# A spectral-filter and Swish kernel: PSUM of the first batch's transform split into five buffers, its stages interleaved per unit, and the second batch moved to other steps

## The chip, the cores and the metric

The kernel runs on one core of a Trainium2 chip. The metric is the device time of one execution in microseconds (us). PE is TensorE, DVE is VectorE, ACT is ScalarE, POOL is GpSimd, SP is SyncE (here it only issues DMAs). Ratios are the mean time of one kernel's fast runs over that of the other kernel's fast runs of the same rounds on the same chip, so they are not quite the ratio of the medians that are quoted beside them. A profile shows one execution; its span is a little shorter than the time of the run.

## The reference, cut to what matters

```python
x:      (8, 3008, 256)          # batch, sequence, channels
filt_r, filt_i: (1505, 256)
w_in:   (256, 2048); w_out: (2048, 256); beta: (2048,)

X = rfft(x, axis=1);  Y = X * (filt_r + 1j*filt_i);  y = irfft(Y, n=3008, axis=1)
h = y.reshape(24064, 256) @ w_in
g = h / (1 + exp(-beta * h))
out = g @ w_out
```

The kernel does both Fourier transforms as matmuls with 3008 = 47 x 64: a stage s1 over 47, a stage s2 over 64, the product with the filter, and the same back (s3, s4).

## The kernel before

The main loop has 752 steps. Each step does two matmuls of the hidden layer (`hps`), the Swish on ACT (`gT`), and, two steps later, four matmuls of the output layer (`acc`). Batch 0 is transformed ahead of the loop ("the setup"). Batches 1 to 7 are transformed inside the loop, their stages spread over the steps by a plan:

```python
first_step = [(S * b // TB) * NFB for b in range(B)] + [NSTEP]     # 0, 80, 176, ...
def at(s, fn, *a):
    plan.setdefault(int(s), []).append((fn, a))
...
if b == 1:                                       # o = 0
    s1_steps(1, range(8, 16), [o + 1 + i for i in range(8)], False)
    for g in range(NH): at(o + 10 + 2 * g, turn_t3, g)
    for g in range(NG): at(o + 12, a2_load, 1, g)
    s23_steps(1, [o + r for r in (20, 23, 26, 29, 33, 36, 39, 42, 45, 50, 53, 56)], 5, True)   # s3 five steps after s2
    for h in range(J // JG): at(o + 64, zz_load, 1, h)
    s4_steps(1, [o + 71 + i // 2 for i in range(16)], True)
    for f in (2, 3):
        at(f, load_wout, f * WG)                 # DMA, issued on SP
        at(f, scale_wout, f * WG)                # POOL
    for g in range(NH): at(4, copy_fr, g)        # two POOL copies each: filt_r on all partitions
    for g in range(4): at(o + 10 + 3 * g, load_x, 2, g)           # DMA, issued on POOL
    late = (57, 58, 59, 60, 61, 62, 66, 67, 68, 69, 70, 71, 72, 73, 74, 75)
    s1_steps(2, range(16), [o + r for r in late], False)
```

The kernel sets a manual schedule, so each engine's instructions stand in the order of the program, and a step of the plan is also a place in each engine's line (POOL's line in the timelines below stands in that order).

```python
def s1(b, i, on_act):            # every fourth unit takes a new a1 tile from a pool of two
    ...
    evac(st["a1", b][:, jj : jj + 2, :], ps[:KP], on_act)          # then a1_store: DMA on SP
def s2(b, i):
    ps, ks = s2_matmuls(b, i)
    nc.vector.tensor_tensor(a_t[:], ps[:], fr_sb[:, ks, :], ALU.mult)          # reads copy_fr's result
    nc.vector.scalar_tensor_tensor(b_t[:M], ps[M:], -1.0, ff_sb[M:, ks, :], ALU.mult, ALU.mult)
    nc.vector.tensor_tensor(b_t[M:], ps[:M], ff_sb[M:, ks, :], ALU.mult)
    nc.gpsimd.tensor_tensor(yh[:], a_t[:], b_t[:], ALU.add)                    # POOL
# s3(b, i): PE multiplies yh; s4 writes y of the batch, which hps reads
```

In the setup, PSUM is one ring of four two-bank buffers, whatever the stage: transposes ("turns"), the two products p and q of a unit (8 frequencies x 128 channels), the return stage.

```python
spsum = tile_pool(name="spsum", bufs=4, space=PSUM)
def s2_0(n):                                     # one unit: both matmul groups, then both products
    ps, pw = bank2([P, KH, P]), bank2([P, KH, P])
    ...
    nc.vector.scalar_tensor_tensor(p_t[:], ps[:], sgn[:], ff_sb[:, ks, ds], ALU.mult, ALU.mult)
    nc.vector.tensor_tensor(q_t[:], pw[:], ff_sb[:, ks, ds], ALU.mult)
```

## Time and profile before

| | before |
|---|---|
| median of 3 runs | 806.81 us (806.59 to 808.27) |
| span of the profile | 803.4 us |
| PE busy | 768.3 us, 96% |
| first `hps` pair of matmuls complete (end of the setup) | 52.4 us |

The page's line of busy times, and from its table of 40 slices (20 us each) the row of PE's busy share in tenths:

```profile
PE 768.3 (96%) x6109; PEld 551.8 (69%) x6201; DVE 448.4 (56%) x694; ACT 556.9 (69%) x807; POOL 169.4 (21%) x186
...
PE   4799997999999999999999999999999999999997
```

(Some matmul records are missing from this trace, 6109 of 6201 are there, so its PE busy time is a little low.) The profiled execution took 805.22 us at a mean clock of 0.998. PE is at 90% or more except in the first two slices (the setup), in the seventh, 120 to 140 us, and in the last. The waits of PE from 45 to 200 us, longest first; each line is who waited, for whom, the total, how often and the longest:

```profile
PE ps L619 <- DVE a L117: 2.2, 1, 2.2
PE ps L619 <- DMA zz<-d: 2.2, 1, 2.2
PE acc L730 <- DVE ost L741: 1.7, 1, 1.7
PE ps L545 <- ACT y L115: 0.9, 1, 0.9
```

Three things cost time there: `zz` (the input of s4) lands late, DVE is late behind an a1 cast (`a`), and the output tile's copy (`ost`) is late. The lines at L619 and L545, with one of 0.3 us left out, make 5.6 us between 126 and 138 us. After 160 us the waits view lists nothing for PE. The chain of waits around the largest gap, in order of time (start, length, what):

```profile
124.60 0.70 DVE a L117
...
125.65 9.93 DMA d<-a
...
135.66 0.69 DVE a L117
136.35 0.46 DVE y L119
```

A store of an a1 tile (`d<-a`) took 9.93 us; the DVE cast that needed the tile's buffer waited for it (4.6 us by DVE's waits), and the `y` of 0.46 us that PE needed stands right behind that cast in the chain, at 136.35 us. After the gaps PE is slow for a while. The windows view (stretch, busy us and instruction count of PE, PEld, DVE, ACT and POOL, granted clock, DMA share, GB/s):

```profile
137.00:138.00 1.00, 0.73 (x7) 0.47 (x5) 0.98 (x3) 0.48 (x1) 0.00 (x0) 0.85 0.19 53
138.00:139.00 1.00, 1.00 (x6) 0.54 (x5) 0.57 (x1) 0.00 (x0) 0.00 (x0) 0.50 0.02 4
141.00:142.00 1.00, 1.00 (x14) 0.71 (x12) 0.34 (x2) 0.12 (x1) 0.00 (x0) 0.95 0.00 0
```

The clock is 0.50 for about 3.4 us, and four `acc` matmuls take 0.85 us there (from 137.84 us) where they took 0.44 before the gaps (from 120.21 us): by an estimate from these two, about 1.7 us of lost work. The longest single gap of PE before it was 2.2 us; what brought the 0.50 on is not shown by this trace.

POOL's line before the second batch (start, length, what, count, idle time before it and what ended that):

```profile
52.91 3.74 POOL L348 TENSOR_TENSOR wout_sb<-ws,rbeta_sb 128x1024 bf16<-128x1024 f32 x2 [3.99 <-DMA ws<-in_moe_w_out_dram]
56.72 1.88 POOL L525 COPY fr_sb<-ff_sb 64x2048 f32<-64x2048 f32 x1
...
66.41 1.89 POOL L526 COPY fr_sb<-ff_sb 64x2048 f32<-64x2048 f32 x1
...
74.99 1.26 POOL L580 TENSOR_TENSOR yh<-a_t,b_t 128x512 bf16<-128x512 f32 x1 [2.48 <-DVE b_t L579]
```

The second pair of w_out scalings (L348) begins when its load lands at 52.9 us, the six copies follow to 68.3 us, and the first `yh` waits for DVE, not for POOL.

### The profile page before, as it was taken

How to read it: one execution, taken by the hardware profiler on the slowest of the kernel's cores; microseconds unless marked ns; L12 is line 12 of the kernel's file. 1: busy time of each engine (PE TensorE's matmuls, PEld its weight loads, DVE VectorE, ACT ScalarE, POOL GpSimd, SP SyncE). 2: the span in 40 equal slices, each digit the busy share in tenths (PEclk: the TensorE clock that was granted, in tenths of full speed). 3: DMA queues.
4: the chain of work that ended last, by engine and by line, in shares of the span. 5: the costliest groups of instructions: out<-in, count | busy, mean ns of one | idle time of the engine just before them, and what ended most of it. 6: DMA issues, size and time to landing. Idle time of an engine off the chain costs nothing.

```text
span 803.4 us, 15446 instructions
## 1 busy us (share of the span) xinstructions
PE 768.3 (96%) x6109; PEld 551.8 (69%) x6201; DVE 448.4 (56%) x694; ACT 556.9 (69%) x807; POOL 169.4 (21%) x186
## 2 busy tenths in 40 slices
PE   4799997999999999999999999999999999999997
PEld 4667664766677666776668766786667766676664
DVE  7665764476655665566655666556764666330101
ACT  4776674776667766676767676677666777777775
POOL 8157331132201322023310222011210122000000
PEclk9999999999999999999999999999999999999999
DMA  9948237523571418513293134912245111500101
GB/s 166 229 135 199 69 80 208 141 74 109 129 219 39 120 47 201 171 49 86 70 244 106 47 86 131 256 33 81 78 135 155 62 58 48 151 27 27 53 28 52
DMA packets 84187, 88.29 MB, mean 110 GB/s; under 512 B 5968, under 2 KB 75088, under 8 KB 83736
## 3 DMA queue, kind: packets, MB, share of 16 engines
q1 hardware_dynamic: 79460, 72.37, 30.2%
q0 software_dynamic: 4656, 14.95, 10.9%
q8 instruction: 48, 0.79, 0.4%
q14 instruction: 23, 0.19, 0.1%
HBM read 54.01 MB, written 46.66 MB: 125 GB/s over the span
## 4 chain that ended last, share of the span: by engine, by line
PE 90%; DMA 1%; DVE 1%; issue 1%; ACT 0%; DVEq 0%; SPq 0%; ACTq 0%
PE acc L730 42%; PE hps L710 38%; PE ps L545 3%; PE ps L590 2%; PE ps L619 2%; PE ps L561 2%; DMA d<-a 1%; DVE a L117 0%; DVE ost L741 0%; PE tp L602 0%; ACT gT L719 0%; DVE a_t L575 0%; DVE b_t L576 0%; DVE b_t L579 0%; DVEq L770 0%
## 5 line engine op out<-in xcount | busy, mean ns | idle before, releaser
L719 ACT ACTIVATE gT<-hps,beta_sb 128x512 bf16<-128x512 f32 x752 | 516.5, 687 | 219.3 <-PE hps L710 196.5
L730 PE MATMUL acc<-wout_sb,gT 128*128 128x256 bf16 x3008 | 454.2, 273 | 4.2 <-DVE ost L741 1.7
L710 PE MATMUL hps<-y,win_sb 128*128 128x512 bf16 (+7 forms) x1636 | 428.6, 350 | 1.2 <-DVE y L119 0.6
L730 PEld LDWEIGHTS <-gT 128*128 128x128 bf16 x3008 | 288.0, 98 | 128.5 <-issue 4.3
L580 POOL TENSOR_TENSOR yh<-a_t,b_t 128x512 bf16<-128x512 f32 x84 | 106.3, 1265 | 426.2 <-DVE b_t L579 419.3
L710 PEld LDWEIGHTS <-win_sb 128*128 128x128 bf16 x1728 | 164.9, 98 | 25.8 <-DVE y L119 1.3
L741 DVE COPY ost<-acc 128x512 f32<-128x512 f32 x94 | 60.5, 685 | 139.8 <-PE acc L730 139.8
L575 DVE TENSOR_TENSOR a_t<-ps,fr_sb 128x512 f32<-128x512 f32 x84 | 58.1, 692 | 75.3 <-PE ps L561 74.7
L117 DVE CAST a<-ps 96x512 bf16<-96x512 f32 x104 | 70.8, 685 | 51.5 <-PE ps L545 44.9
L119 DVE TENSOR_SCALAR y<-ps 128x376 bf16<-128x376 f32 x104 | 55.9, 547 | 61.4 <-PE ps L619 61.2
L576 DVE SCALAR_TENSOR_TENSOR b_t<-ps,ff_sb 64x512 f32<-64x512 f32 x84 | 58.2, 692 | 1.1
L579 DVE TENSOR_TENSOR b_t<-ps,ff_sb 64x512 f32<-64x512 f32 x84 | 57.4, 683 | 1.1
L117 DVE CAST z<-ps 128x512 bf16<-128x512 f32 x78 | 53.4, 684 | 1.8 <-PE ps L590 0.8
L619 PEld LDWEIGHTS <-zz 96*128 96x128 bf16 x448 | 29.5, 99 | 27.1 <-issue 3.3
L545 PE MATMUL ps<-xg,t 94*96 94x512 bf16 x104 | 40.0, 384 | 1.9 <-ACT y L115 0.9
L619 PE MATMUL ps<-t,zz 96*128 96x94 bf16 x448 | 34.4, 206 | 5.2 <-DVE a L117 2.2
L590 PE MATMUL ps<-yh,t 128*128 128x256 bf16 x168 | 32.1, 273 | 0.6
L561 PE MATMUL ps<-a,tw_sb 128*128 128x256 bf16 x168 | 32.1, 273 | 0.3
L590 PEld LDWEIGHTS <-t 128*128 128x128 bf16 x168 | 16.3, 98 | 17.7 <-issue 0.2
L335 POOL DMA_DIRECT2D xg<-in_x_dram x28 | 15.1, 539 | 62.7 <-PE ps L545 57.4
L561 PEld LDWEIGHTS <-tw_sb 128*128 128x128 bf16 x168 | 16.1, 98 | 16.3
L545 PEld LDWEIGHTS <-t 94*96 94x96 bf16 x104 | 12.9, 124 | 10.1 <-DVE b_t L579 0.4
(94 smaller groups left out, 218.3 us busy)
## 6 DMA issues: line engine op xcount, KB each, us to landing
out_dram<-ost SPq DMA_DIRECT2D x47, 512.0 KB, 3.0
d<-a SPq DMA_DIRECT2D x28, 384.0 KB, 3.3
a<-d SPq DMA_DIRECT2D x28, 384.0 KB, 5.1
d<-z SPq DMA_DIRECT2D x28, 384.0 KB, 3.7
zz<-d SPq DMA_DIRECT2D x28, 384.0 KB, 6.7
xg<-in_x_dram POOLq DMA_DIRECT2D x28, 320.0 KB, 6.2
ws<-in_moe_w_out_dram SPq DMA_DIRECT2D x4, 512.0 KB, 5.3
xg<-in_x_dram POOLq DMA_DIRECT2D x28, 56.0 KB, 6.0
```

Source lines behind the costliest of these rows:

```text
L117: nc.vector.tensor_copy(dst, src)
L545: nc.tensor.matmul(ps[:KP], lhsT=t1[:], rhs=xg[b, g][:, jj : jj + 2, :], start=True, stop=True)
L561: nc.tensor.matmul(ps[:, e, :], lhsT=t2[:, k0 + e, :], rhs=st["a2", b, g][:, kk + e, :], start=True, stop=True,)
L575: nc.vector.tensor_tensor(a_t[:], ps[:], fr_sb[:, ks, :], ALU.mult)
L576: nc.vector.scalar_tensor_tensor(b_t[:M], ps[M:], -1.0, ff_sb[M:, ks, :], ALU.mult, ALU.mult)
L580: nc.gpsimd.tensor_tensor(yh[:], a_t[:], b_t[:], ALU.add)
L590: nc.tensor.matmul(ps[:, e, :], lhsT=t3[:, 2 * i + e, :], rhs=yh[:, e, :], start=True, stop=True)
L619: nc.tensor.matmul(ps[:, e, :NP], lhsT=zz[:, j0 % JG + e, dc * P : (dc + 1) * P], rhs=t4[:], start=True, stop=True,)
L710: nc.tensor.matmul(hps[:, pos - t0 : pos - t0 + ln], lhsT=win_sb[:, dc, fb * P : (fb + 1) * P], rhs=ys[b][:, dc, n0 : n0 + ln], start=(dc ...
L719: nc.scalar.activation(gT[:], hps[:], ACT.Silu, scale=beta_sb[:, fb : fb + 1])
L730: nc.tensor.matmul(acc[tb // 2][:, tb % 2, :], lhsT=gT[:, tb * P : (tb + 1) * P], rhs=wout_sb[:, fb, :], start=(fb == 0 and tb % 2 == 0), ...
L741: nc.vector.tensor_copy(ost[:, 2 * h : 2 * h + 2, :], acc[h][:])
```

## The change

Its intent: let the setup's products on DVE follow each other by giving the short turns their own one-bank PSUM buffers and by putting a turn or a return stage between the p and the q matmuls of a unit; and let the second batch start earlier, with its s1, s2, s3, s4 and the third batch's s1 on steps that do not collide (s4 on steps 67 to 79 instead of 71 to 78), and two of its s1 casts, those of units 10 and 14, on ACT instead of DVE. The core of the diff:

```diff
-        tc.tile_pool(name="spsum", bufs=4, space=bass.MemoryType.PSUM)
+        tc.tile_pool(name="spsum", bufs=3, space=bass.MemoryType.PSUM)
+    )
+    tpsum = right.enter_context(
+        tc.tile_pool(name="tpsum", bufs=2, space=bass.MemoryType.PSUM)
...
+    def turn8():
+        return tpsum.tile([P, KH, P], BF16, name="tps", tag="tps")
...
-    s2_0(0)
-    a0_turn(1, (False, True))
-    t3_part(1, 1, True)
-    t3_part(0, 1, True)
-    s2_0(1)
-    s3_0(0)
...
+    s2_0(1, False)          # p of unit 1
+    t3_part(0, 1)
+    s2_0(1, True)           # q of unit 1
+    s3_0(0)
+    t3_part(1, 1)
+    a0_turn(2, 0, False)
...
-            s1_steps(1, range(8, 16), [o + 1 + i for i in range(8)], False)
+            s1_steps(1, range(8, 16), [o + r for r in (0, 1, 1, 2, 3, 4, 4, 5)], False, (10, 14))
...
-                at(o + 10 + 2 * g, turn_t3, g)
+                at(o + 6 + 3 * g, turn_t3, g)
-                at(o + 12, a2_load, 1, g)
-            s23_steps(1, [o + r for r in (20, 23, 26, 29, 33, 36, 39, 42, 45, 50, 53, 56)], 5, True)
+                at(o + 8, a2_load, 1, g)
+            s23_steps(1, [o + r for r in (15, 18, 21, 24, 27, 30, 34, 37, 40, 43, 46, 50)], 5, True)
-                at(o + 64, zz_load, 1, h)
-            s4_steps(1, [o + 71 + i // 2 for i in range(16)], True)
+                at(o + 59, zz_load, 1, h)
+            s4_steps(1, [o + 67 + (i * 12) // 15 for i in range(16)], True)
...
-                late = (57, 58, 59, 60, 61, 62, 66, 67, 68, 69, 70, 71, 72, 73, 74, 75)
+                late = (54, 55, 56, 57, 58, 59, 60, 61, 66, 67, 68, 70, 72, 73, 74, 76)
```

Untouched are the plan's lines for `load_wout`, `scale_wout`, `copy_fr` and `load_x` of the third batch. Two of the second batch's four-unit groups are still transformed in the setup, but four of their eight units now come after the last product instead of two of eight.

More of the change, by code (lines that the diff above doesn't have):

```diff
@@ L241, in s1_0, with a0_turn, t3_part @@
         evac(aTv[:, g], src, on_act)
-    def a0_turn(kg, acts):
-        tp = bank2([P, KH, NDC, P], BF16)
-        ks = slice(kg * KH, (kg + 1) * KH)
+    def a0_turn(kg, e, on_act):
+        tp = turn8()
         for kk_ in range(KH):
-            for e in range(NDC):
-                k2 = 2 * (kg * KH + kk_)
-                nc.tensor.transpose(
-                    tp[:, kk_, e, :], aT[:, e, k2 : k2 + 2, :].rearrange("p c m -> p (c m)"), ident[:]
-                )
-        hk = KH // 2
-        for n, on_act in enumerate(acts):
-            evac(
-                a0[:, kg * KH + n * hk : kg * KH + (n + 1) * hk, :],
-                tp[:, n * hk : (n + 1) * hk].rearrange("p k e d -> p k (e d)"),
-                on_act,
-            )
-    def t3_part(c, g, on_act):
-        tp = bank2([P, 2 * KH, P], BF16)
+            k2 = 2 * (kg * KH + kk_)
+            nc.tensor.transpose(
+                tp[:, kk_, :], aT[:, e, k2 : k2 + 2, :].rearrange("p c m -> p (c m)"), ident[:]
+            )
+        evac(a0[:, kg * KH : (kg + 1) * KH, e * P : (e + 1) * P], tp[:], on_act)
+    def t3_part(c, g, on_act=True):
+        tp = turn8()
         ks = slice(g * KH, (g + 1) * KH)
@@ L266, in t3_part @@
             )
-        evac(t3c[:, c, ks, :], tp[:, :KH, :], on_act)
+        evac(t3c[:, c, ks, :], tp[:], on_act)
     def dup(dst, src):
@@ L281 @@
     t2_part(1, 1)
-    dup(0, 1)
     s1_0(4, False)
     s1_0(5, True)
-    t3_part(0, 0, True)
     nc.vector.memset(t2[:, 0, M : P : M - 1], 0.0)
+    dup(4, 1)
     s1_0(6, False)
     s1_0(7, True)
+    dup(0, 1)
     dup(3, 2)
-    dup(4, 1)
     n1s = small("n1s")
@@ L299 @@
     nc.vector.tensor_scalar(sgn[:], c_i[:], -2.0, 1.0, ALU.mult, ALU.add)
+    a0_turn(0, 0, False)
+    a0_turn(0, 1, True)
     kkf, c4f, qqf = (t[:].rearrange("p a b c -> p (a b c)") for t in (kk, c4, qq))
@@ L306 @@
     nc.scalar.activation(sn[:], kkf, ACT.Sin, scale=TWO_PI / TURN)
-    a0_turn(0, (False, True))
     nc.vector.scalar_tensor_tensor(
@@ L310 @@
     )
-    t3_part(1, 0, True)
     r_sq.close()
@@ L364, with z_turn @@
     y_tile(0)
-    JT = 16
-    def z_turn(e, hh, acts):
-        tp = bank2([P, JT, P], BF16)
-        for i in range(JT):
-            j0 = (hh * JT + i) * KP
+    def z_turn(e, hh, on_act):
+        tp = turn8()
+        for i in range(KH):
+            j0 = (hh * KH + i) * KP
             nc.tensor.transpose(tp[:, i, :], zT[e][:, j0 : j0 + P], ident[:])
-        hj = JT // 2
-        for n, on_act in enumerate(acts):
-            js = slice(hh * JT + n * hj, hh * JT + (n + 1) * hj)
-            evac(zz0[:, js, e * P : (e + 1) * P], tp[:KP, n * hj : (n + 1) * hj, :], on_act)
+        evac(zz0[:, hh * KH : (hh + 1) * KH, e * P : (e + 1) * P], tp[:KP], on_act)
     def s4_0(e, hh, on_act):
@@ L397, with s2_0 @@
     p0pool = rpool("p0pool", r_p0, bufs=2)
-    def s2_0(n):
+    def s2_0(n, swapped):
         kg, e = units[n]
         ds = slice(e * P, (e + 1) * P)
-        ps, pw = bank2([P, KH, P]), bank2([P, KH, P])
-        for dst, col in ((ps, M), (pw, 3 * M)):
-            for kk_ in range(KH):
-                k1 = kg * KH + kk_
-                nc.tensor.matmul(
-                    dst[:, kk_, :],
-                    lhsT=tw_sb[:, k1, col : col + P],
-                    rhs=a0[:, k1, ds],
-                    start=True,
-                    stop=True,
-                )
-        ks = slice(kg * KH, (kg + 1) * KH)
-        p_t = p0pool.tile([P, KH, P], BF16, name="p_t", tag="p_t")
-        q_t = p0pool.tile([P, KH, P], BF16, name="q_t", tag="q_t")
-        nc.vector.scalar_tensor_tensor(
-            p_t[:], ps[:], sgn[:], ff_sb[:, ks, ds], ALU.mult, ALU.mult
-        )
-        nc.vector.tensor_tensor(q_t[:], pw[:], ff_sb[:, ks, ds], ALU.mult)
-        pq[n] = (p_t, q_t)
+        ks = slice(kg * KH, (kg + 1) * KH)
+        ps = bank2([P, KH, P])
+        col = 3 * M if swapped else M
+        for kk_ in range(KH):
+            k1 = kg * KH + kk_
+            nc.tensor.matmul(
+                ps[:, kk_, :], lhsT=tw_sb[:, k1, col : col + P], rhs=a0[:, k1, ds], start=True, stop=True
+            )
+        r_t = p0pool.tile([P, KH, P], BF16, name="pq_t", tag=f"pq{int(swapped)}")
+        if swapped:
+            nc.vector.tensor_tensor(r_t[:], ps[:], ff_sb[:, ks, ds], ALU.mult)
+        else:
+            nc.vector.scalar_tensor_tensor(
+                r_t[:], ps[:], sgn[:], ff_sb[:, ks, ds], ALU.mult, ALU.mult
+            )
+        pq[n, swapped] = r_t
     def s3_0(n):
         kg, e = units[n]
-        p_t, q_t = pq.pop(n)
         ps = bank2([P, KH, P])
-        for kk_ in range(KH):
-            k1 = kg * KH + kk_
-            for c, src in enumerate((p_t, q_t)):
+        for c in range(2):
+            src = pq.pop((n, c == 1))
+            for kk_ in range(KH):
                 nc.tensor.matmul(
@@ L431, in s3_0 @@
                     lhsT=src[:, kk_, :],
-                    rhs=t3c[:, c, k1, :],
-                    start=c == 0,
+                    rhs=t3c[:, c, kg * KH + kk_, :],
+                    start=c == 0 and kk_ % 4 == 0,
                     stop=c == 1,
+                    skip_group_check=True,
                 )
@@ L444 @@
     units = [(0, 0), (0, 1), (1, 0), (2, 0), (1, 1), (2, 1)]
-    for g in range(2):
+    for g in range(3):
         load_x(1, g)
     nc.gpsimd.dma_start(win_sb[:], moe_w_in.rearrange("(dc p) f -> p dc f", p=P))
-    for g in range(2, 4):
-        load_x(1, g)
+    load_x(1, 3)
     load_wout(0)
@@ L453, with s1_early @@
         nc.gpsimd.memset(zT[e][:, WZ:], 0.0)
-    def s1_pair(n):
-        g, hb = divmod(n, 2)
-        if hb == 0:
+    def s1_early(i, on_act):
+        g, jj = divmod(2 * i, JG)
+        if jj == 0:
             st["a1", 1] = apool.tile([KP, JG, D], BF16, name="a1", tag="a1")
-        ps = bank2([P, 4, D])
-        for e in range(2):
-            nc.tensor.matmul(
-                ps[:KP, 2 * e : 2 * e + 2, :],
-                lhsT=t1[:],
-                rhs=xg[1, g][:, 4 * hb + 2 * e : 4 * hb + 2 * e + 2, :],
-                start=True,
-                stop=True,
-            )
-        evac(st["a1", 1][:, 4 * hb : 4 * hb + 4, :], ps[:KP], True)
-        if hb == 1:
-            a1_store(1, g)
@@ L472 @@
-    s2_0(0)
-    a0_turn(1, (False, True))
-    t3_part(1, 1, True)
-    t3_part(0, 1, True)
-    s2_0(1)
-    s3_0(0)
-    a0_turn(2, (False, True))
-    tp4 = bank2([P, 2 * KH, P], BF16)
-    nc.tensor.transpose(tp4[:KP, 0, :NP], t1[:], ident[:NP, :NP])
-    nc.scalar.activation(t4[:], tp4[:KP, 0, :NP], ACT.Copy)
-    nc.gpsimd.tensor_scalar(t4[0:4], t4[0:4], 0.5, None, ALU.mult)
-    s2_0(2)
-    s3_0(1)
-    t3_part(0, 2, True)
-    t3_part(1, 2, True)
-    s2_0(3)
-    s3_0(2)
-    s1_pair(0)
@@ L490, with turn_t4 @@
-    s1_pair(1)
-    warm = small("warm")
-    nc.scalar.activation(warm[:], ms[:], ACT.Silu)
-    s2_0(4)
-    s3_0(3)
-    s1_pair(2)
-    z_turn(0, 0, (True, True))
-    s2_0(5)
+        ps = tpsum.tile([P, 2, D], F32, name="tps", tag="tps")
+        nc.tensor.matmul(
+            ps[:KP], lhsT=t1[:], rhs=xg[1, g][:, jj : jj + 2, :], start=True, stop=True
+        )
+        evac(st["a1", 1][:, jj : jj + 2, :], ps[:KP], on_act)
+        if jj + 2 == JG:
+            a1_store(1, g)
+    def turn_t4():
+        tp = turn8()
+        nc.tensor.transpose(tp[:KP, 0, :NP], t1[:], ident[:NP, :NP])
+        nc.scalar.activation(t4[:], tp[:KP, 0, :NP], ACT.Copy)
+        nc.gpsimd.tensor_scalar(t4[0:4], t4[0:4], 0.5, None, ALU.mult)
@@ new lines @@
+    warm = small("warm")
+    s2_0(0, False)
+    t3_part(0, 0)
+    s2_0(0, True)
+    t3_part(1, 0)
+    nc.scalar.activation(warm[:], ms[:], ACT.Silu)
+    a0_turn(1, 0, False)
+    s2_0(1, False)
+    t3_part(0, 1)
+    s2_0(1, True)
+    s3_0(0)
+    t3_part(1, 1)
+    a0_turn(2, 0, False)
+    s2_0(2, False)
+    t3_part(0, 2)
+    s2_0(2, True)
+    s3_0(1)
+    t3_part(1, 2)
+    a0_turn(1, 1, False)
+    s2_0(3, False)
+    turn_t4()
+    s2_0(3, True)
+    s3_0(2)
+    s1_early(0, True)
@@ L498 @@
+    a0_turn(2, 1, False)
+    s2_0(4, False)
+    s1_early(1, True)
+    s2_0(4, True)
+    s3_0(3)
+    s1_early(2, True)
+    s1_early(3, True)
+    s2_0(5, False)
+    z_turn(0, 0, True)
+    s2_0(5, True)
     s3_0(4)
-    z_turn(0, 1, (False, False))
+    z_turn(0, 1, True)
+    z_turn(0, 2, False)
     s3_0(5)
+    z_turn(0, 3, False)
+    s4_0(0, 0, False)
+    s4_0(0, 1, True)
     tiny = sp.tile([P, NFB], F32, name="tiny", tag="tiny")
@@ L508 @@
     scale_wout(WG)
-    s4_0(0, 0, True)
-    s4_0(0, 1, False)
-    s1_pair(3)
-    z_turn(1, 0, (False, True))
-    z_turn(1, 1, (False, True))
-    s4_0(0, 2, True)
-    s4_0(0, 3, False)
-    for hh in range(J // JG):
-        s4_0(1, hh, hh % 2 == 0)
+    s1_early(4, False)
+    s1_early(5, True)
+    z_turn(1, 0, False)
+    z_turn(1, 1, True)
+    s4_0(0, 2, False)
+    z_turn(1, 2, False)
+    z_turn(1, 3, True)
+    s4_0(0, 3, True)
+    s4_0(1, 0, False)
+    s4_0(1, 1, True)
+    s1_early(6, False)
+    s1_early(7, True)
+    s4_0(1, 2, False)
+    s4_0(1, 3, True)
     r_p0.close()
@@ L633, in at, with s1_steps @@
         plan.setdefault(int(s), []).append((fn, a))
-    def s1_steps(b, units_, steps, act):
+    def s1_steps(b, units_, steps, act, on_act=()):
         assert len(steps) == len(units_)
         for i, s in zip(units_, steps):
-            at(s, s1, b, i, act and i % 2 == 1)
+            at(s, s1, b, i, i in on_act)
             if i % 4 == 3:
```

## The prediction

> **What bounds it.** The page gives a span of 803.4 us, PE busy 96%, the chain of waits 90% PE. PE's idle time sits in few places (chain and waits by stretch): the first batch's own transform before the first hidden-layer matmul, at 51.0 us; 1.7 us at 86.8 us (acc waits for the DVE copy of ost, queued behind a 2.1 us unit); 126 to 138 us: 2.2 us for zz to land, 2.2 us for DVE, which sat 4.6 us on an a1 buffer whose store took 9.9 us, and smaller waits, some 5.8 us in all. Then the granted clock is 0.50 from 138 to 141 us (about 1.6 us lost). After 160 us PE waits for nothing. [...]
>
> **Setup.** Work is unchanged; only order and buffers change. From 21.8 us to the first hidden matmul DVE had about 23 us and ACT 23 us of work in 29 us. Evacuating the a0 turns moves to DVE. Chaining durations of the trace through the new buffers (f32 products 1.28 and 1.21 us, bf16 copies 0.69 DVE or 1.02 ACT, 8 transposes 0.45) I get units every 3.2 us instead of 3.9, and the last q product ends about 40.4 instead of 43.6 us. But the tail gets longer: two of the second batch's pairs fall into it and eight z turns pass through two one-bank buffers: 11 us against 8. First hidden matmul near 50 to 51.5 us: -1 us.
>
> **Second batch, gains.** No unit now stands on step 33, so ost is not delayed: -1.7. Twelve steps instead of ten lie between the last s3 and the first s4, and the late s1 stores are spread: -5.5, and the half-clock stretch goes: -1.6. The last s4 moves to step 79, one before its reader: +0.6.
>
> **A new stall.** On SP, in program order, the third a1 store (units 8 to 11, now complete at step 2) stands before the two last w_out loads; before they stood ahead of it and were issued at 47.8 us. Now they go out near 56 and land near 61 (5.1 us). [...] two scalings (1.9 us each), six fr copies (11.6 us; before 56.7 to 68.3), now ending near 76; two x loads (2.2 us); only then the first yh of the second batch, done near 80. But s2 moved from step 20 to 15, and the first s3 stands at step 20, where PE arrives near 73. So PE waits about 7 us at the first s3, which costs a half-clock stretch too, +1.6; perhaps +0.5 at step 10 for w_out. The stall eats what the other steps win.
>
> **Sum.** -1 -1.7 -5.5 -1.6 +0.6 +7 +1.6 +0.5 = about 0. Predicted 806.5 us, 800 to 811. Chances: faster by over 2% 0.03, within 2% 0.94, slower 0.03.
>
> **Signs.** Right if: the waits of PE show ps of s3 waiting for POOL yh, several us near 73 to 80 us, a clock of 0.5 after it; the w_out loads issue after 54 us; the fr copies end after 74; no PE wait near ost before 100 us; little PE idle before step 80; first hidden matmul at 49.5 to 51.5 us. PE's busy time away from half-clock stretches is unchanged.
>
> **Wrong if:** the tail of the setup overlaps better than my chain says (2 to 4 us more gained), the w_out loads come earlier than I read from the order of the program, in which case the stall shrinks and it ends near 798; or zz and the a1 stores still collide near step 67 to 72.

The terms add up to -0.1 us, which the prediction calls about 0. The -1.6 and the +1.6 for half-clock stretches are estimates from the clock of 0.50 between 138 and 141 us in the trace before; that such a stretch would come with the new gap was not shown by that trace, and is by the one of the changed kernel below (0.50 from 76 to 82 us). One figure is high: from 21.8 to 51.0 us DVE was busy for 21.3 us, not about 23.

## The result

| | before | changed |
|---|---|---|
| median | 806.81 us | 803.63 us (802.75 to 803.70) |
| ratio | | 0.9952, 95% interval 0.9930 to 0.9975 |
| span of the profile | 803.4 us | 801.0 us |
| first `hps` pair complete | 52.4 us | 50.6 us |

The same views of the changed kernel (helper lines have moved: `hps` is L722, `acc` L742, s3 L602, s4 L631, w_out scaling L345, copies L537 and L538, `yh` L592):

```profile
PE 771.9 (96%) x6201; PEld 551.8 (69%) x6201; DVE 449.5 (56%) x696; ACT 554.7 (69%) x809; POOL 169.6 (21%) x186
...
PE   4886999999999999999999999999999999999997
```

```profile
PE ps L602 <- POOL yh L592: 6.7, 1, 6.7
...
PE acc L742 <- DVE ost L753: 0.4, 1, 0.4
...
PE acc L742 <- POOL wout_sb L345: 0.3, 1, 0.3
```

The last step of the setup is in the table; the last q product of the setup (DVE, start and length) and the `hps` matmul that completes the first pair (PE; the line of the kernel before holds the next one too) show where its 1.8 us come from, first before, then changed:

```profile
42.43 1.21 DVE L419 TENSOR_TENSOR q_t<-sps,ff_sb 128x1024 bf16<-128x1024 f32 x1
...
52.01 0.82 PE L710 MATMUL hps<-y,win_sb 128*128 128x512 bf16 x2 [0.63 <-DVE y L119]
```

```profile
38.63 1.23 DVE L405 TENSOR_TENSOR pq_t<-sps,ff_sb 128x1024 bf16<-128x1024 f32 x1 [0.48 <-PE sps L400]
...
50.22 0.38 PE L722 MATMUL hps<-y,win_sb 128*128 128x512 bf16 x1 [0.80 <-ACT y L115]
```

The products end 3.8 us earlier (39.9 against 43.6 us), and 2 us of that are given back by a longer tail (10.4 us against 8.4, to the start of the `hps` matmul that completes the first pair).

In the loop the waits for `zz` and for the a1 cast are gone, that for `ost` fell from 1.7 to 0.4 us, and one long new wait, of 6.7 us, stands in their place: s3 waits for POOL's `yh`. The chain of waits shows what it is made of:

```profile
52.37 0.70 DVE a L117
...
53.12 0.30 SPq L320
...
53.52 5.79 DMA ws<-in_moe_w_out_dram
...
59.38 1.44 POOL wout_sb L345
...
63.19 1.89 POOL fr_sb L537
...
70.92 1.89 POOL fr_sb L537
...
75.89 0.52 POOL xg L332
...
76.93 1.28 POOL yh L592
...
78.25 0.58 PE ps L602 x2
```

Read from the top: the DVE cast that completes the third a1 group, SP issuing that group's store (L320) and only then the w_out load, which lands 5.79 us later; two scalings, the copies, two x loads, the first `yh`, and at 78.25 us PE's s3. The first `yh`'s inputs were ready from DVE at 69.1 us, but it started at 76.93 us, after the copies and the two x loads that stand before it in POOL's part of the program (the first of the three DVE products that make its inputs had itself waited 2.6 us for the first two copies, until 67.0 us). POOL's line, to compare with the one before:

```profile
59.38 3.74 POOL L345 TENSOR_TENSOR wout_sb<-ws,rbeta_sb 128x1024 bf16<-128x1024 f32 x2 [12.06 <-DMA ws<-in_moe_w_out_dram]
63.19 1.89 POOL L537 COPY fr_sb<-ff_sb 64x2048 f32<-64x2048 f32 x1
...
72.87 1.89 POOL L538 COPY fr_sb<-ff_sb 64x2048 f32<-64x2048 f32 x1
...
76.93 1.27 POOL L592 TENSOR_TENSOR yh<-a_t,b_t 128x512 bf16<-128x512 f32 x1
```

And the clock after the gap, where it fell while PE was still idle:

```profile
75.00:76.00 1.00, 0.00 (x0) 0.00 (x0) 0.00 (x0) 0.00 (x0) 1.00 (x3) 0.65 0.00 0
78.00:79.00 1.00, 0.75 (x4) 0.55 (x4) 0.12 (x1) 0.00 (x0) 1.00 (x3) 0.50 1.15 205
80.00:81.00 1.00, 1.00 (x6) 0.52 (x5) 0.00 (x0) 0.36 (x1) 1.00 (x3) 0.50 1.06 193
82.00:83.00 1.00, 1.00 (x8) 0.67 (x7) 0.99 (x2) 0.44 (x1) 0.00 (x0) 0.94 0.97 172
```

From 78.25 to about 82 us PE worked at 0.50 (four `acc` matmuls took 0.85 us from 78.84 us on), by an estimate from the 3.8 us about 1.9 us lost. So the change swapped two gaps and a half-clock stretch near 130 us (5.6 and 1.7 us) for one gap and a half-clock stretch near 75 us (6.7 and 1.9 us).

### The profile page after: what moved, and what is told of

Read it like the earlier page. It is cut to its first block, busy times and chain, and to the rows that moved or that the text cites. A ratio compares the mean times of both kernels' runs of the same rounds, so it can differ in the third digit from the quotient of the medians.

```text
span 801.0 us, 15536 instructions
## 1 busy us (share of the span) xinstructions
PE 771.9 (96%) x6201; PEld 551.8 (69%) x6201; DVE 449.5 (56%) x696; ACT 554.7 (69%) x809; POOL 169.6 (21%) x186
## 4 chain that ended last, share of the span: by engine, by line
PE 91%; DMA 3%; POOL 2%; ACT 1%; DVE 1%; issue 1%; SPq 0%; DVEq 0%; POOLq 0%; ACTq 0%
PE acc L742 40%; PE hps L722 40%; PE ps L557 3%; PE ps L631 2%; PE ps L602 2%; PE ps L573 2%; DMA ff_sb<-in_filt_i_dram 1%; DMA x<-in_x_dram 1%; DMA ws<-in_moe_w_out_dram 1%; POOL fr_sb L537 1%; PE sps L418 1%; POOL fr_sb L538 0%; PE tps L367 0%; POOL wout_sb L345 0%; ACT y L115 0%
## 5 line engine op out<-in xcount | busy, mean ns | idle before, releaser
L742 PE MATMUL acc<-wout_sb,gT 128*128 128x256 bf16 x3008 | 454.2, 273 | 0.7 <-DVE ost L753 0.4
L722 PE MATMUL hps<-y,win_sb 128*128 128x512 bf16 (+7 forms) x1728 | 448.9, 352 | 1.0 <-ACT y L115 1.0
L742 PEld LDWEIGHTS <-gT 128*128 128x128 bf16 x3008 | 287.9, 98 | 125.6 <-issue 2.6
L592 POOL TENSOR_TENSOR yh<-a_t,b_t 128x512 bf16<-128x512 f32 x84 | 106.3, 1265 | 415.5 <-DVE b_t L591 408.6
L722 PEld LDWEIGHTS <-win_sb 128*128 128x128 bf16 x1728 | 165.1, 98 | 25.1 <-DVE y L119 0.8
L631 PEld LDWEIGHTS <-zz 96*128 96x128 bf16 x448 | 29.7, 98 | 22.9
L602 PE MATMUL ps<-yh,t 128*128 128x256 bf16 x168 | 32.3, 274 | 6.7 <-POOL yh L592 6.7
L631 PE MATMUL ps<-t,zz 96*128 96x94 bf16 x448 | 34.7, 205 | 0.0
L602 PEld LDWEIGHTS <-t 128*128 128x128 bf16 x168 | 16.3, 98 | 24.5 <-issue 6.9
```

The source lines that it names most:

```text
L602: nc.tensor.matmul(ps[:, e, :], lhsT=t3[:, 2 * i + e, :], rhs=yh[:, e, :], start=True, stop=True)
L631: nc.tensor.matmul(ps[:, e, :NP], lhsT=zz[:, j0 % JG + e, dc * P : (dc + 1) * P], rhs=t4[:], start=True, stop=True,)
L722: nc.tensor.matmul(hps[:, pos - t0 : pos - t0 + ln], lhsT=win_sb[:, dc, fb * P : (fb + 1) * P], rhs=ys[b][:, dc, n0 : n0 + ln], start=(dc ...
L742: nc.tensor.matmul(acc[tb // 2][:, tb % 2, :], lhsT=gT[:, tb * P : (tb + 1) * P], rhs=wout_sb[:, fb, :], start=(fb == 0 and tb % 2 == 0), ...
```

## The experiments

Theory: the new stall is POOL's line being late, because the w_out loads moved behind the third a1 store on SP and because s2 moved five steps forward; the setup gained about 2 us. Rivals: the stall comes from elsewhere (a2, DVE, the new setup), or the setup made the gain. All kernels below gave correct results.

### Copies at step 0 (`copy_first`, `copy_first_again`)

```diff
-                at(4, copy_fr, g)
+                at(0, copy_fr, g)
```
(on the changed kernel)

> The changed kernel with one number changed: the six fr copies stand at step 0 instead of step 4, so ahead of the two last w_out scalings in GpSimd's order, where GpSimd sat idle from 47.3 to 59.4 us. Theory (the new stall at the first s3 is GpSimd's backlog behind the late w_out loads): copies end near 59, scalings near 63, first yh near 70, PE's wait for yh (6.7 us) and the half-clock stretch after it (about 1.6 us) vanish: about 795 us, ratio 0.986. Rival (the stall is due to a2 landing late or to DVE's product units): the wait at the first s3 stays and the time stays at 803 to 804.

Measured: median 793.73 us (792.36 to 794.03) beside 807.54 of the kernel before, ratio 0.9832 (0.9813 to 0.9851). The copies now fill the time in which POOL had waited for the load:

```profile
46.33 1.88 POOL L537 COPY fr_sb<-ff_sb 64x2048 f32<-64x2048 f32 x1
...
57.88 3.74 POOL L345 TENSOR_TENSOR wout_sb<-ws,rbeta_sb 128x1024 bf16<-128x1024 f32 x2
...
67.55 1.26 POOL L592 TENSOR_TENSOR yh<-a_t,b_t 128x512 bf16<-128x512 f32 x1 [3.78 <-DVE b_t L591]
```

The first `yh` again waits for DVE. The waits of PE from 45 to 200 us are down to the setup's own:

```profile
PE hps L722 <- ACT y L115: 1.0, 2, 0.8
PE sps L373 <- ACT y L115: 0.3, 1, 0.3
```

Neither a wait for `yh` nor a half-clock stretch is left (the mean clock is 1.00 in every stretch of the windows view, from 0 to 180 us). The stall and what followed it are shown to be POOL's backlog, and this version beats both kernels. It was run once more as the comparison for the last three experiments:

> The kernel with the copies at step 0 once more, as the comparison for the three runs beside it: ratio 0.983, as in its first run; first hidden matmul complete near 50 us.

Measured: 794.38 us (793.31 to 796.16), ratio 0.9851 (0.9822 to 0.9879).

### The two halves of the change (`setup_only`, `steps_only`)

Edits: the changed kernel's setup with the old plan, and the old setup with the changed plan (the last hunk of the diff above, out or in as a whole).

> The changed first batch (buffers, interleaving) with the old steps of the second batch. Theory: the first hidden matmul's second half comes at 50.2 us instead of 52.0, nothing else gained, stalls near 87 and 126 to 138 us stay: about 805 us, ratio 0.998. There is no yh stall, since the old steps leave it until step 25. Rival (the setup is what brought the gain of the changed kernel): 803.6, ratio 0.995.

Measured: 806.01 us, ratio 0.9986 (0.9967 to 1.0005). The old waits (zz, 2.6 us, and ost, 1.7 us) are there. A wait of 0.7 us for `yh`, which the expectation had ruled out, appears too: the w_out loads are 1.9 us later here as well (issued at 49.7 us instead of 47.8), and all four x loads stand ahead of the first `yh` in POOL's line, which reached it at 74.5 us. The interval includes 1, so this half is not shown to gain; its profile shows the fastest of its seven runs (802.18 us; the other six took 805.22 us or more).

> The old first batch with the new steps of the second batch. Theory: the stalls at 87 and 126 to 138 us go, with the half-clock stretch (about 9 us gained), and the yh stall at the first s3 appears, 6 to 7 us, with its own half-clock stretch: about 805.5 us, ratio 0.998. Rival (the yh stall comes from the new setup's timing, not from the steps): no such stall, 797 to 798 us, ratio 0.989.

Measured: 804.99 us, ratio 0.9976 (0.9958 to 0.9994), and the stall is there with the old setup too:

```profile
PE ps L590 <- POOL yh L580: 6.7, 1, 6.7
```

So the stall comes from the steps. The steps alone gain about 0.2%; the setup alone is at 0.1%, which is not clear of the noise.

### The w_out loads ahead of the third a1 store (`loads_first`)

```diff
+            for f in (2, 3):
+                at(0, load_wout, f * WG)
             s1_steps(1, range(8, 16), ...)
...
             for f in (2, 3):
-                at(f, load_wout, f * WG)
                 at(f, scale_wout, f * WG)
```

> The changed kernel with the two last w_out loads issued ahead of the third a1 store on SP, as the old order had them. Theory: they go out near 50 us instead of 53.5, land 3.5 us earlier, and all of GpSimd's line moves up by 3.5 us: PE's wait for the first yh falls from 6.7 to about 3.2 us[...]: 799 to 800 us, ratio 0.991. Rival (copies, not loads, are what GpSimd's lateness is made of): less than 1 us gained.

Measured: 798.30 us (795.62 to 800.20), ratio 0.9887 (0.9865 to 0.9910). The loads were issued at 49.6 us instead of 53.5, and the wait fell as computed:

```profile
PE ps L602 <- POOL yh L592: 3.2, 1, 3.2
```

```profile
74.00:75.00 1.00, 1.00 (x6) 0.74 (x5) 0.69 (x1) 0.00 (x0) 0.98 (x3) 0.50 1.10 209
75.00:76.00 1.00, 1.00 (x5) 0.41 (x3) 0.00 (x0) 0.01 (x1) 1.00 (x2) 0.50 1.12 225
```

With the wait of 3.2 us a half-clock stretch came all the same (0.53 from 73 to 74 us, then 0.50 to 76 us and 0.76 to 77 us), about 3 us of it after PE had resumed. The 3.5 us alone lead from 803.6 to about 800 us. The runs spread over 4.6 us, more than those of the kernel without the stall (1.7 and 2.9 us in its two groups). The clocks go with it: the two fastest runs (795.62 and 795.82 us) have a mean clock of 0.998, the other four 0.995 or 0.996. So the mean clock differs from run to run; where it differs is not shown, since only one of them has a profile.

### The x loads later (`x_later`, `x_later_again`)

```diff
-                    at(o + 10 + 3 * g, load_x, 2, g)
+                    at(o + 22 + 3 * g, load_x, 2, g)
```

> The changed kernel with the four x loads of the third batch moved from steps 10 to 19 to steps 22 to 31, so that two of them (2.2 us of GpSimd's issue time) no longer stand between the copies and the first yh. Theory (GpSimd's line ahead of the first yh is a plain sum): PE's wait for yh falls from 6.7 to about 4.5 us, the half-clock stretch stays (in the run with the loads first, a wait of 3.2 us still brought it): about 801.4 us, ratio 0.993. Rival (yh is late for another reason): no change, 803.6.

Measured: five of six runs at 799.46 to 802.12 us, ratio of the fast runs 0.9912 (0.9897 to 0.9928). The sixth, the one with the profile, took 1648.25 us: PE was busy 99% of it at about half the pace (401 matmuls from 400 to 500 us, 770 in the changed kernel; 443 ns for one of `acc`, 273 elsewhere), while its clock record says 1.000. Nothing about this kernel can be read from that profile, so it was run again:

> The kernel with the x loads moved later, once more, since its profile fell in an execution of 1648 us that says nothing about the kernel. Theory as before: PE's wait for the first yh is 4.5 us where it was 6.7, with a half-clock stretch after it, ratio about 0.992. Rival: 6.7 us as in the changed kernel.

Measured: 799.04 us, ratio 0.9900 (0.9868 to 0.9932), and the wait:

```profile
PE ps L602 <- POOL yh L592: 4.4, 1, 4.4
```

From 6.7 to 4.4 us: the issue time of two x loads (2.2 us) came out of the line, as a sum would have it, and the clock still fell (0.89 on average from 70 to 85 us, by an estimate from that about 3.3 us at 0.50). The three edits of POOL's line (copies, w_out loads, x loads) take 6.7, 3.5 and 2.3 us off the wait.

### The wait for ost (`unit_32`)

```diff
-            s23_steps(1, [o + r for r in (20, 23, 26, 29, 33, 36, ...
+            s23_steps(1, [o + r for r in (20, 23, 26, 29, 32, 36, ...
```
(on the kernel before)

> The kernel before with one unit of the second batch moved from step 33 to step 32. Theory (ost was late only because that unit's three DVE products, 2.07 us, stand before it in the step where the block ends): PE's wait of 1.7 us for ost near 87 us goes or falls under 0.7 us: ratio 0.998 to 0.999. Rival (DVE is late at the block's end in any case): the wait stays, ratio 1.000.

Measured: 805.38 us beside 807.73, ratio 0.9973 (0.9955 to 0.9990). The wait fell to 0.8 us, a little above the bound of 0.7 that was set:

```profile
PE acc L730 <- DVE ost L741: 0.8, 1, 0.8
```

The cause holds; part of the wait stays with one step's distance. The medians differ by 2.4 us, more than the 0.9 us that the wait fell; the rest is not explained.

### Only the third batch's s1 steps (`late_only`)

```diff
-                late = (57, 58, 59, 60, 61, 62, 66, 67, 68, 69, 70, 71, 72, 73, 74, 75)
+                late = (54, 55, 56, 57, 58, 59, 60, 61, 66, 67, 68, 70, 72, 73, 74, 76)
```
(on the kernel before, nothing else)

> The kernel before with only the third batch's first-stage units on the changed kernel's steps (54 to 61 and 66 to 76 in place of 57 to 75). Theory (one of the two gaps near 126 to 138 us is the a1 buffer's store, the other the late landing of zz): DVE's 4.6 us wait on the a1 store and PE's 2.2 us behind it go, the 2.2 us wait for zz stays[...]: about 4 us gained, ratio 0.995. Rival (both gaps come from zz landing late, the stores being a by-product): less than 1 us gained.

Measured: 799.86 us (799.34 to 800.13) beside 807.73, ratio 0.9900 (0.9885 to 0.9915): 7.9 us, twice what was expected, and more than the whole change brought. In the profile DVE waits for no a1 store from 100 to 145 us, the clock is whole from 125 to 145 us, and PE's waits there are down to one:

```profile
PE acc L730 <- DVE ost L741: 1.7, 1, 1.7
PE ps L619 <- DMA zz<-d: 1.1, 1, 1.1
```

The expectation: its 4 us were the wait of 2.2 us and the estimate of the half-clock stretch (about 1.7 us, from the trace before), which is gone here; why it is gone is not shown. The theory names the larger cause rightly and missed in size. Of the 3.9 us beyond the expectation the profiles show 2.0: the wait for zz fell too (from 2.2 to 1.1 us), and that of 0.9 us for `y` is gone. The rest is not in these two profiles; a likely part of it, not shown, is that the profiled execution of the kernel before was milder than the eleven beside this run (806.37 to 809.81 us, clocks of 0.992 to 0.996). Why zz came less late here was not tested. This line of 16 numbers alone is worth more than the change that it is part of, and the rest of that change put the `yh` stall in.

### The shape of PSUM (`one_pool`, `pools_2_4`)

Both are edits of the kernel with the copies at step 0, run beside it on one chip.

```diff
-        tc.tile_pool(name="spsum", bufs=3, ...)      tpsum: bufs=2      # as changed
+        tc.tile_pool(name="spsum", bufs=4, ...)      no tpsum           # one_pool: turns from the two-bank ring
+        tc.tile_pool(name="spsum", bufs=2, ...)      tpsum: bufs=4      # pools_2_4
```

> The kernel with the copies at step 0, the new interleaving kept, but PSUM in the old shape: one ring of four two-bank buffers for all stages of the first batch. Theory (the interleaving, which lets DVE go from product to product, brought most of the setup's 1.8 us; the split only gives one buffer more): the last q product ends about where it does with the split (39.9 us) or up to 1 us later, and the first hidden matmul comes less than 1 us later. Rival (the split matters: in one ring, turns wait for the slow products ahead of them): the setup gets 2 us or more longer and the gain over the old setup is lost.

Measured: 794.26 us, ratio 0.9845 (0.9820 to 0.9870), against 0.9851 for the split beside it: no difference. In the profiles the last q product ends at 41.2 us instead of 39.9, but the tail is shorter by as much: the `hps` matmul that completes the first pair starts at 50.42 us, with the split at 50.24. So the new order of the setup (the interleaving, with what it moves between DVE and ACT) does the work; the split, on its own, bought nothing that these runs can resolve. Which part of the order counts was not tested.

> The kernel with the copies at step 0 and PSUM split into two two-bank and four one-bank buffers instead of three and two. Theory (the tail after the last product is held by the two one-bank buffers): the tail gets shorter by 1 us or more, but with two buffers for p, q and z the next product's matmuls wait for DVE, and the middle loses more: first hidden matmul 1 to 3 us later than with three and two. Rival (the one-bank buffers are the limit all along): the setup gets shorter.

Measured: 797.12 us, ratio 0.9878 (0.9852 to 0.9905), in the medians 2.7 us slower than three and two beside it (the fastest run is 0.8 us under the slowest of those). PE waits for the products, four times in a row:

```profile
PE sps L418 <- DVE pq_t L407: 3.7, 4, 1.1
```

Two buffers for p, q and the return stage are one too few. Against the theory, the tail did not get shorter: from the last q product (which ended at 40.8 us) to the `hps` matmul that completes the first pair it took 10.6 us, against 10.4 with three and two; it was held by ACT's y (1.1 us).

### The filters' first group first (`filters_first`)

```diff
             lo = eng is nc.sync
+            eng = nc.sync if g else eng            # groups 1 and 2: all on SP, behind group 0
...
+    nc.gpsimd.dma_start(seen2[:], ff_sb[:1, 0, :2])   # holds POOL's x loads until group 0 has landed
```
(on the kernel with the copies at step 0)

> The kernel with the copies at step 0, with the first group of filter loads ahead of the others: groups 1 and 2 all issued on SP behind group 0, and GpSimd's x loads held until group 0 has landed. Theory (the first p product, at 21.9 us, waits 1.4 us for the filter's load, and everything after it in the setup follows): p starts 1 to 1.3 us earlier and the first hidden matmul 0.5 to 1.3 us earlier: ratio 0.982. Rival (a later load, group 1 or the second batch's x, takes over as the limit): no gain, or a loss of up to 2 us.

Measured: 797.56 us, ratio 0.9885 (0.9859 to 0.9911), a loss of about 3 us. DVE's products of units 2 and 3 (start, length, what, count, idle before):

```profile
27.26 1.28 DVE L408 SCALAR_TENSOR_TENSOR pq_t<-sps,sgn,ff_sb 128x1024 bf16<-128x1024 f32 x1
...
34.37 1.28 DVE L408 SCALAR_TENSOR_TENSOR pq_t<-sps,sgn,ff_sb 128x1024 bf16<-128x1024 f32 x1 [3.41 <-PE sps L401]
```

The first product did start earlier (20.5 us, against 21.5 in the profile beside it), but that of unit 3, the first to use group 2, started at 34.37 us instead of 30.98. The view puts its idle time down to a PE matmul that had ended before; the last filter load was issued at 19.0 us, took the longest of all to land, 15.3 us, and so landed at 34.3 us. So the rival holds, with the last load, that of group 2, as the limit. The loop began about 3 us later: its first casts of a1 on DVE (two in the view's line) started at 53.88 us, with the filters in the old order at 50.93. In the first profile of the kernel with the copies at step 0 the filters happened to land earlier and the first product started at 20.0 us: this wait differs from run to run by more than a microsecond.

## Why the prediction was right

The measured 803.63 us lies in the range, and the class (within 2%) was right; the sum was 2.9 us too high. The number alone proves little, since a forecast of no change at all would have lain in the range too; what was foreseen is the swap of one stall for another.

- **The new stall** was read from the order of the program alone: forecast about 7 us with a half-clock stretch of 1.6 us, measured 6.7 and about 1.9 us. That it is so close is partly luck: POOL's and PE's times were both forecast 1.5 to 2.5 us too late (loads issued near 56, measured 53.5; first `yh` done near 80, measured 78.2; PE at s3 near 73, measured 71.5), and the errors cancel in the difference. Its causes are confirmed step by step: SP's order by `loads_first`, POOL's line by `copy_first` and `x_later_again`, the new steps as a whole by `steps_only`. The earlier step of s2 was not tried alone.
- **The signs:** the copies ended at 74.8 us (forecast: after 74), and the clock of 0.50 came. Two signs missed by 0.5 us: the w_out loads went out at 53.5 us (after 54 forecast), the first `hps` matmul started at 49.05 us (49.5 to 51.5 forecast). "No PE wait near ost" missed by 0.4 us: that unit of DVE's line had itself been held by the late copies. PE's busy time can't be compared, since 92 matmul records of the kernel before are missing.
- **The setup** was mis-sized: forecast -1 us, measured -1.8 us. The last product ended at 39.9 us (forecast 40.4), and the tail took 10.4 us (forecast 11).
- **The gaps near 130 us**: forecast -5.5 and -1.6 us; in the profile these waits (5.6 us) went, and the half-clock stretch (1.7 us). **The wait for ost**: forecast -1.7, measured -1.3 us. `late_only` shows that most of what the gaps cost (4.3 of the 5.6 us of waits, and the stretch) belongs to one line of the change. The rest, twelve steps between s3 and s4 instead of ten, was not tested alone.
- **The last s4 at step 79**: forecast +0.6, measured 0.2 us. **w_out at step 10**: forecast +0.5, measured 0.3 us.

The setup (0.8), s4 (0.4), w_out (0.2) and ost (-0.4) make 1 us of the 2.9. The other 1.9 us is not assigned to a step; the kernel before itself varies more than that (803.15 to 809.23 us within one group of runs), and its profiled execution, on which the prediction rests, was 1.6 us faster than the median that the sum starts from.

## What to carry to other kernels

When a stage is moved forward in a software pipeline, look at the line of every engine that feeds it, with the work of other stages that stands ahead of it in the order of the program: here six copies, two w_out loads and two x loads that the diff does not touch, behind one store that it moves ahead of the w_out loads, and a first `yh` that started 7.8 us after its inputs were ready (76.93 and 69.1 us). Try the parts of a schedule change one at a time: one line of it was worth 7.9 us, the whole 3 to 4, and one number more made that 12 to 14. POOL's 12.06 us of idle time before the second scalings looked harmless, but it was the place for work that is needed later and could be done then.

## What these runs show of the clock and of an x load, and leave open

- The clock fell to 0.50 about 1.3 us after the last of three gaps of 2.2, 0.9 and 2.2 us within ten microseconds (kernel before: 0.85 from 137 to 138 us, then 0.50), in a gap of 3.2 us (`loads_first`: 1.00 from 72 to 73 us, 0.53 from 73 to 74), and about 4 us into a gap of 6.7 us (changed kernel: 1.00 from 74 to 75 us, 0.65 from 75 to 76). In `setup_only`, where the longest wait of PE between 45 and 200 us is 2.6 us, for zz, it was 0.91 on average from 125 to 145 us. In the profiles of `late_only` and `unit_32` it was 0.66 on average from 51 to 56 us, at the start of the loop (`late_only`: 0.50 from 52 to 54 us), where the waits view shows no gap of PE over 0.7 us just before; the other profiles have 1.00 there. What brings it on is left open. After PE had resumed, the stretch took about 3 to 4 us to end (3.4 us in the kernel before, about 3.8 in the changed one), but about 5.5 us in `steps_only` (from 79.5 us on: 0.50 up to 84 us, 0.83 on average from 80 to 95).
- The clock record did not show the pace of every execution: one of `x_later` ran at about half pace from end to end (1648 us, 443 ns for a matmul of 273) with a recorded clock of 1.000.
- An x load (two DMAs with a cast, about 6 us each to landing) held POOL's line for 1.04 to 1.19 us (0.65 and 0.54, then 0.53 and 0.51 us, from 74.71 us on in the changed kernel), with no tensor instruction of POOL in that time, and two of them were 2.2 us of a 6.7 us stall.
